# Written order instead of scheduled order: the queues of TensorE, ScalarE and VectorE in the MLP's stage of an attention and MLP kernel

## Chip, cores and metric

The kernel runs on one core of a Trainium2 chip. The metric is the device time of one execution in microseconds (us), the median of several runs. Half a per cent is about what runs of this kernel tell from no change.

Short names, as in the profile: PE is TensorE (matmuls), PEld its weight loads, ACT is ScalarE, DVE is VectorE, POOL is GpSimd, SP is SyncE, which issues the transfers (DMA).

## What is computed

Two attention blocks through 32 inducing points for each of 4 batches of 12480 rows of 128 values, and then an MLP with squared ReLU over all 49920 rows:

```python
def mab(q, kv):
    s = scale * (q @ kv.transpose(0, 2, 1))
    s = s - s.max(-1, keepdims=True)
    a = np.exp(s)
    a /= a.sum(-1, keepdims=True) + 1e-09
    return a @ kv
h = mab(I, x)                 # 32 inducing rows attend to all rows of x
x = mab(x, h)                 # each row of x attends to the 32 rows of h
hid = x.reshape(B * S, D) @ w_in          # 128 -> 2048
out = np.square(np.maximum(hid, 0)) @ w_out   # 2048 -> 128
```

## The kernel before

A row of the second attention is a mixture of the 32 rows of `h`, so the MLP's input has only 32 free values per row. The kernel uses that: per batch it prepares small matrices from `h`, `w_in` and `w_out`, and the MLP's 2048 hidden units become 512 squares of pair differences (four blocks of 128) and a linear part. An exact version for inputs on which this would not be close enough stands at the end, behind a switch, and is not taken here.

Per batch there are these pieces of work, each written as a Python generator whose `yield` ends a *step*:

- `first(b)`: the first attention. Seven groups of scores (four column groups side by side on PE, VectorE scales them into `sT` and takes maxima), the maximum's way across partitions (`mt`, `mb`, ending in `nb`), exponentials of `sT` on ACT, then for each of seven groups a transpose `en` on VectorE, a reduction `xm` over `xT` on VectorE, 30 small matmuls `hacc` on PE and a sum `hq` on VectorE; at the end `hs` and `ht`, which give `hT`.
- `prepare(b)`: 23 steps from `hT` to the MLP's matrices. PE: `hwv` (two halves of 8 blocks), `am`, `bc`, `R`, `pl`, `rb`, `cat`, `w` and four times `wq`; between any two of them VectorE has small work, and ACT evicts `hwv` and `wq` and casts `hws` (to `hw16`), `hwS` and `hot` (to `g4`).
- `second(b, G)`: the second attention for one of seven groups of columns: scores on PE, transpose and maximum on VectorE, a subtraction on POOL, the exponential on ACT, sum and reciprocal on VectorE, a multiplication on POOL, the transpose back, the narrowing to f16 on ACT or VectorE, a transfer to DRAM (`ad`) and back in another layout (`dT`).
- `squares(b, G)`: one small product per chunk (`sq`), squared on POOL (`zz`), which fills the last 32 rows of `dT`.
- 26 chunks of 480 columns: `up(j)` makes half j (two blocks of 128) of the pair differences on PE into `hp`; `lift(j)` squares that half on ACT into `g` (one instruction on 128 x 960); `down()` multiplies the four blocks of `g` by `w16` and adds the linear part into `po`, which ACT or VectorE evicts to `o`, and SP sends out.

PSUM holds two `hp` buffers (two banks each), two `po` and two for everything else (`att_psum`). Which of ACT and VectorE does an eviction is decided by `to_act` from two running sums of estimated work, `held`.

The program loops over the 104 chunks of all batches in order. After each half chunk, `background(k)` gives the next steps that are due: of `second` up to three groups ahead of the chunk, of `first` and `prepare` of the *next* batch so that they end with this batch's last chunks, and of `squares`. The order in which instructions are written is only a priority: a list scheduler puts each engine's queue in the order in which its own forecast has them ready. Before the loop, `first(0)` runs between the narrowing of the weights (`weights()`, a step of it at those steps of `first(0)` that `WHEN` lists), then `prepare(0)` with the first two groups of `second`.

Of the kernel before, what the change touches and what calls it, by code (L numbers as in the profile page):

```python
# [36 lines left out]
WHEN = (0, 2, 4, 8, 10, 12, 14)  # L37
# [3 lines left out]
def attend_then_relu2_mlp(ctx: ExitStack, tc: tile.TileContext, xn, xT, indT, w_in, w_out, outT):  # L41
# [20 lines left out]
    scale = 1.0 / math.sqrt(P)  # L62

# [15 lines left out]
    for k in range(2):  # L79
        nc.vector.tensor_reduce(fold[:, k], ident.rearrange("p (q i) -> p i q", q=4), axis=AX.X, op=ALU.add)  # L80
    rep = const.tile([P, 4, MI], F32, name="rep")
    nc.vector.tensor_copy(rep, fold[:, 0:1].broadcast_to([P, 4, MI]))
    ones = const.tile([1, P], F32, name="ones")
    nc.vector.memset(ones, 1.0)
    onec = const.tile([P, NF], F32, name="onec")
    nc.vector.memset(onec, 1.0)
# [3 lines left out]
    nc.vector.tensor_copy(slot, slot_i)  # L90

    late = const.tile([P, 1], F32, name="late")
    nc.vector.tensor_reduce(late, ident[:, 112:P], axis=AX.X, op=ALU.add)
    sgn = const.tile([P, NQ], F32, name="sgn")
    nc.vector.memset(sgn, -1.0)
    nc.vector.tensor_scalar(sgn[:, 3:4], late, 2.0, -1.0, op0=ALU.mult, op1=ALU.add)

    cut = const.tile([P, 1], F32, name="cut")
    nc.vector.tensor_reduce(cut, fold[:, 0, 0:16], axis=AX.X, op=ALU.add)
    nc.vector.tensor_scalar(cut, cut, -3e38, None, op0=ALU.mult)  # L100
    lessen = const.tile([P, 1], F32, name="lessen")
    nc.vector.memset(lessen, -(2.0 ** 14) / MI)
    part = const.tile([MI, 1], F32, name="part")
    nc.vector.memset(part, (2.0 ** 14) / MI)

    pairs = const.tile([P, NQ * P], F16, name="pairs")
    nc.vector.memset(pairs, 0.0)
    fold_f = fold.rearrange("p k i -> p (k i)")
    for s in range(1, 17):
        n = MI if s < 16 else 16  # L110
        nc.vector.tensor_tensor(
            pairs[0:64, MI * (s - 1):MI * (s - 1) + n], fold_f[0:64, 0:n], fold_f[0:64, s:s + n], op=ALU.subtract,
        )
    nc.vector.tensor_copy(pairs[0:64, 31 * 16:32 * 16], fold_f[0:64, 0:16])
# [11 lines left out]
    for k in range(2):  # L126
# [7 lines left out]
        nc.vector.memset(one.singles, 0.0)  # L134
        nc.vector.tensor_copy(one.singles[0:64, 0:16], fold[0:64, 0, 16:MI])
# [23 lines left out]
    def evac(dst, src, cols, by=None):  # L159

        if to_act(120 + 0.833 * cols, 110 + 1.042 * cols):
            if by is None:
                nc.scalar.copy(dst, src)
            else:
                nc.scalar.mul(dst, src, by)
        elif by is None:
            nc.vector.tensor_copy(dst, src)
        else:
            nc.vector.tensor_scalar(dst, src, by, None, op0=ALU.mult)
# [10 lines left out]
    def all_max(col, name):  # L180

        tp = att_psum(f"{name}_t")
        nc.tensor.transpose(tp[0:1, 0:P], col, ident)
        m = work.tile([1, 1], F32, tag="am_m", name=f"{name}_m")
        nc.vector.tensor_reduce(m, tp[0:1, 0:P], axis=AX.X, op=ALU.max)
        nc.vector.tensor_scalar(m, m, 2.0 ** -60, None, op0=ALU.max)
        yield
        bp = att_psum(f"{name}_b")
        nc.tensor.matmul(bp[:, 0:1], ones, m, start=True, stop=True)
        p2 = work.tile([P, 1], F32, tag="am_p", name=f"{name}_p", bufs=4)  # L190
        nc.vector.tensor_copy(p2, bp[:, 0:1])
        nc.vector.tensor_scalar(p2.bitcast(I32), p2.bitcast(I32), 0x7F800000, None, op0=ALU.bitwise_and)
# [7 lines left out]
    def narrow(dst, wd, name):  # L200
# [5 lines left out]
        nc.vector.tensor_scalar(a, hi, 3, 0x3FFFFFFF, op0=ALU.logical_shift_left, op1=ALU.bitwise_and)  # L206
        nc.vector.scalar_tensor_tensor(a, hi, 0xC0000000, a, op0=ALU.bitwise_and, op1=ALU.bitwise_or)
        nc.vector.tensor_scalar(m, a, 0xFF800000, None, op0=ALU.bitwise_and)
        nc.vector.scalar_tensor_tensor(r, lo, 2.0 ** -52, m.bitcast(F32), op0=ALU.mult, op1=ALU.mult)
        nc.vector.tensor_tensor(r, a.bitcast(F32), r, op=ALU.add)  # L210
        nc.vector.tensor_scalar(m, hi, 0x7FFFFFFF, None, op0=ALU.bitwise_and)
        nc.vector.scalar_tensor_tensor(dst, m, float(0x38100000), r, op0=ALU.is_ge, op1=ALU.mult)
# [3 lines left out]
    def prepare_w_out():  # L216
        m = small("wmax")
        nc.vector.tensor_reduce(m, wm4, axis=AX.X, op=ALU.max)
        p2 = yield from all_max(m, "wo")
        nc.vector.tensor_scalar(inv_t, p2, 2.0 ** -14, None, op0=ALU.mult)  # L220
        t = small("wt")
        nc.vector.reciprocal(t, inv_t)
        nc.scalar.mul(w_hi, wo_sb, t)
        yield
# [9 lines left out]
    def scores(ps, lhsT, xp, w):  # L234
        for q in range(4):
            nc.tensor.matmul(  # L236
# [3 lines left out]
    def first(b):  # L240
# [3 lines left out]
        nc.vector.memset(sT[:, NCH * TP:NCH * TP + 16], 0.0)  # L244
        mx = work.tile([P, NG], F32, tag="mx", name=f"mx_{b}")
        for G, w in enumerate(WID):
            if b:
                st.xp[G] = load_xT(b, G)
                yield
            ps = att_psum(f"s1_{b}_{G}")  # L250
            xg = st.xp[G]
            scores(ps, indT_sb, xg, w)
            held["dve"] += 150 + 1.042 * w
            nc.vector.tensor_scalar(
                sT[:, 480 * G:480 * G + w], ps[:, 0:w], scale, None, op0=ALU.mult, op1=ALU.max, accum_out=mx[:, G:G + 1],
            )
            yield

# [15 lines left out]
        xns = {h: load_xn(h) for h in range(XB)}  # L274
        m1 = small("m1")
        nc.vector.tensor_reduce(m1, mx, axis=AX.X, op=ALU.max)
        tp = att_psum(f"mt_{b}")
        nc.tensor.transpose(tp[0:1, 0:P], m1, ident)
        gm = work.tile([1, MI], F32, tag="gm", name=f"gm_{b}")
        nc.vector.tensor_reduce(gm, tp[0:1, 0:P].rearrange("a (q i) -> a i q", q=4), axis=AX.X, op=ALU.max)  # L280
        gm4 = work.tile([1, 4, MI], F32, tag="gm4", name=f"gm4_{b}")
        nc.vector.tensor_copy(gm4, gm.unsqueeze(1).broadcast_to([1, 4, MI]))
        yield
        bp = att_psum(f"mb_{b}")
        nc.tensor.matmul(bp[:, 0:1], gm4.rearrange("a q i -> a (q i)"), ones[:, 0:1], start=True, stop=True)
        nb = small("nb")
        nc.vector.tensor_scalar(nb, bp[:, 0:1], -1.0, None, op0=ALU.mult)  # L287
        yield

        def largest(G):  # L290
            held["dve"] += 60 + 1.042 * 4 * WID[G]
            nc.vector.tensor_reduce(  # L292
# [3 lines left out]
        def exp(G):  # L296
# [3 lines left out]
            nc.scalar.activation(s, s, AF.Exp, bias=nb, accum_out=zs[:, G:G + 1])  # L300
# [6 lines left out]
        for G, nb32 in enumerate(BLK):  # L307
            en = work.tile([P, 15, MI], F32, tag="en", name=f"en_{b}_{G}")
            held["dve"] += 110 + 1.042 * 32 * nb32
            nc.vector.transpose(  # L310
                en[:, 0:nb32].rearrange("p t i -> p (t i)"), sT[:, 480 * G:480 * G + 32 * nb32],
            )
# [3 lines left out]
            yield  # L316
            hacc = att_psum(f"hacc_{b}_{G}")
            for t in range(nb32):
# [4 lines left out]
                st.last = nc.tensor.matmul(  # L323
# [4 lines left out]
            if G == 0:  # L328
                nc.vector.tensor_copy(hq[:, 0:P], hacc[:, 0:P])
            else:  # L330
                nc.vector.tensor_tensor(hq[:, 0:P], hacc[:, 0:P], hq[:, 0:P], op=ALU.add)  # L331
            if G == NG - 1:
                nc.vector.tensor_reduce(hq[:, P:P + 1], zs, axis=AX.X, op=ALU.add)
            yield
        hs = att_psum(f"hs_{b}")
        nc.tensor.matmul(hs[:, 0:P + 1], rep.rearrange("p q i -> p (q i)"), hq, start=True, stop=True)
        zr = small("zr")
        nc.vector.tensor_scalar(zr, hs[:, P:P + 1], 1e-9, None, op0=ALU.add)
        nc.vector.reciprocal(zr, zr)
        nc.vector.tensor_scalar(st.hn, hs[:, 0:P], zr, None, op0=ALU.mult)  # L340
        yield
        ht = att_psum(f"ht_{b}")
        nc.tensor.transpose(ht[:, 0:P], st.hn, ident)
        nc.vector.tensor_copy(st.hT[:, 0:P], ht[:, 0:P])
        nc.vector.tensor_reduce(st.hT[:, P:P + 1], ht[:, 0:MI], axis=AX.X, op=ALU.add)
        nc.vector.tensor_scalar(st.hT[:, P:P + 1], st.hT[:, P:P + 1], 1.0 / MI, None, op0=ALU.mult)
        yield

    def second(b, G, again=False):
# [6 lines left out]
        if wb > w:  # L356
            nc.vector.memset(ps[:, w:wb], 0.0)  # L357
# [4 lines left out]
        nc.vector.transpose(ef[:, 0:wb], ps[:, 0:wb])  # L362
# [577 lines left out]
```

## Time and profile before

| | |
|---|---|
| time, median of 3 runs | 578.0 us (576.37 to 578.41) |
| the profiled execution's own time | 579.12 us |
| its span, first to last instruction | 577.3 us |
| mean granted TensorE clock | 0.869 of full speed |
| busy: PE, VectorE, ACT, POOL | 438.9, 365.3, 296.8, 83.4 us |
| weight loads (PEld, beside PE) | 204.5 us |

How to read it: one execution on the chip is profiled. Busy time is the sum of an engine's instructions; the granted clock is what the power and activity throttle allowed TensorE, 1.00 being full speed. A row of a group names the kernel's line, the engine, the operation, what it writes and reads, the count, the busy us and mean ns of one, and then the idle time of the engine just before these instructions and what ended it. In a row of the time order the first number is the start, the second the length, both in us; `x4` counts merged instructions.

### The profile page before, as it was taken

The page shows a single profiled execution, that of the slowest core. Times are in us where ns is not written, and L with a number is a line of the kernel's source. Part 1 is how long each engine was busy: PE and PEld are TensorE (multiplying, and loading weights), DVE is VectorE, ACT ScalarE, POOL GpSimd, SP SyncE. Part 2 cuts the span into 40 slices and gives each one's busy share as a digit, 9 for nine tenths or more (in the row PEclk, how much of TensorE's full clock was granted, in tenths as well). Part 3 has the DMA queues.
Part 4 walks back from the last instruction along what each step waited for, and adds up shares of the span by engine and source line. Part 5 has one row for each costly group of instructions (what it writes and reads, how often), then busy time and mean ns, then how long its engine had stood idle before and what let it go on. Part 6 is the DMA issues. An engine that isn't in the chain of part 4 may idle for free.

```text
span 577.3 us, 8820 instructions
## 1 busy us (share of the span) xinstructions
PE 438.9 (76%) x3083; PEld 204.5 (35%) x3083; DVE 365.3 (63%) x947; ACT 296.8 (51%) x419; POOL 83.4 (14%) x93
## 2 busy tenths in 40 slices
PE   1615465777798889769878899769777999897882
PEld 0014334522233536413333545313243555223330
DVE  6999758662555268997254298985534378767342
ACT  0030112437577266747875376628574476565771
POOL 0000011030211010242021021222011022422010
PEclk9999655997789569989889799969969599899997
DMA  8958715024528606565867535735866332334543
GB/s 322 399 214 277 277 69 154 1 86 155 179 80 305 199 20 226 172 182 167 280 226 230 178 102 186 270 104 145 311 211 190 107 105 72 97 126 130 168 132 131
DMA packets 64590, 100.82 MB, mean 175 GB/s; under 512 B 22800, under 2 KB 53776, under 8 KB 64528
## 3 DMA queue, kind: packets, MB, share of 16 engines
q1 hardware_dynamic: 64528, 100.08, 52.1%
q8 instruction: 28, 0.46, 0.3%
q14 instruction: 34, 0.28, 0.2%
HBM read 64.91 MB, written 31.95 MB: 168 GB/s over the span
## 4 chain that ended last, share of the span: by engine, by line
PE 44%; DVE 28%; ACT 13%; issue 6%; DMA 3%; POOL 3%; SPq 1%; POOLq 0%; ACTq 0%; DVEq 0%
PE po L654 10%; PE hp L639 9%; ACT g L648 8%; PE s L236 7%; DVE xm L292 5%; PE hwv L448 5%; PE hacc L323 4%; DVE G L605 3%; DMA outT_dram<-o 2%; PE po L655 2%; PE wq L611 2%; ACT o L658 2%; DVE e L362 2%; PE R L529 2%; DVE z L372 2%
## 5 line engine op out<-in xcount | busy, mean ns | idle before, releaser
L648 ACT ACTIVATE g<-hp 128x960 f16<-128x960 f32 x208 | 193.2, 970 | 87.9 <-PE hp L639 48.9
L639 PE MATMUL hp<-dT,pairs 96*128 96x480 f16 x416 | 122.0, 385 | 29.0 <-ACT g L648 28.1
L654 PE MATMUL po<-g,w 128*128 128x480 f16 x416 | 119.4, 399 | 16.1 <-ACT o L658 6.0
L368 POOL TENSOR_TENSOR e<-e,mx 128x480 f32<-128x480 f32 (+1 forms) x28 | 26.5, 947 | 334.8 <-DVE mx L364 222.8
L639 PEld LDWEIGHTS <-pairs 96*128 96x128 f16 x416 | 37.8, 99 | 97.6 <-issue 75.7
L654 PEld LDWEIGHTS <-w 128*128 128x128 f16 x416 | 41.1, 104 | 75.4 <-issue 43.9
L292 DVE TENSOR_REDUCE xm<-xp_False 128x1 f32<-128x1920 f32 (+1 forms) x28 | 55.7, 1989 | 5.3 <-DMA xp_False<-xT_dram 5.3
L658 ACT ACTIVATE o<-po,bias,osc 128x480 f32<-128x480 f32 x66 | 48.9, 753 | 18.9 <-PE po L655 7.1
L236 PE MATMUL s<-xp_False,indT_sb 128*32 128x480 f32 (+1 forms) x224 | 37.7, 743 | 20.5 <-DMA xp_False<-xT_dram 12.3
L323 PE MATMUL hacc<-xnb,en 128*32 128x128 f32 x784 | 39.2, 328 | 17.2 <-issue 9.3
L655 PE MATMUL po<-dT,lin 128*128 128x480 f16 x104 | 42.3, 408 | 2.7 <-DMA dT<-zz 2.7
L432 POOL TENSOR_TENSOR zz<-z 128x480 f16<-128x480 f32 (+1 forms) x28 | 28.9, 1030 | 87.8 <-DVE z L428 72.1
L660 DVE TENSOR_SCALAR o<-po,osc,bias 128x480 f32<-128x480 f32 x38 | 28.7, 767 | 18.0 <-DMA outT_dram<-o 6.8
L323 PEld LDWEIGHTS hacc<-xnb,en 128*32 128x32 f32 x784 | 26.7, 129 | 34.3 <-issue 20.1
L300 ACT ACTIVATE sT<-sT,nb 128x480 f32<-128x480 f32 (+1 forms) x28 | 18.2, 653 | 35.5 <-DVE nb L287 35.5
L236 PE MATMUL s<-xp_False,hT 128*32 128x480 f32 (+1 forms) x224 | 34.5, 628 | 2.1 <-DVE s L357 1.7
L375 POOL TENSOR_TENSOR e<-e,z 128x480 f32<-128x480 f32 (+1 forms) x28 | 27.6, 986 | 53.8 <-DVE z L374 48.6
L428 DVE TENSOR_SCALAR z<-sq,off,cut 128x480 f32<-128x480 f32 (+1 forms) x28 | 21.4, 764 | 21.8 <-PE sq L422 21.7
L605 DVE TENSOR_TENSOR G<-hwp,hw 128x512 f16<-128x512 f16 x64 | 30.1, 510 | 5.0 <-PE wq L611 4.7
L369 ACT ACTIVATE e<-e 128x480 f32<-128x480 f32 (+1 forms) x28 | 16.1, 574 | 31.6 <-POOL e L368 31.6
L362 DVE STREAM_TRANSPOSE e<-s 128x480 f32<-128x480 f32 (+1 forms) x28 | 18.0, 644 | 15.4 <-PE s L236 14.9
L331 DVE TENSOR_TENSOR hq<-hacc,hq 128x128 f32<-128x128 f32 x24 | 6.8, 284 | 33.0 <-PE hacc L323 33.0
(208 smaller groups left out, 498.6 us busy)
## 6 DMA issues: line engine op xcount, KB each, us to landing
outT_dram<-o SPq DMA_DIRECT2D x104, 240.0 KB, 2.2
xp_False<-xT_dram SPq DMA_DIRECT2D x24, 960.0 KB, 5.8
xnb<-xn_dram SPq DMA_DIRECT2D x28, 448.0 KB, 6.1
xnb<-xn_dram SPq DMA_DIRECT2D x24, 512.0 KB, 5.8
dT<-ad SPq DMA_DIRECT2D x72, 120.0 KB, 2.7
ad<-a SPq DMA_DIRECT2D x24, 240.0 KB, 2.7
dT<-zz SPq DMA_DIRECT2D x104, 30.0 KB, 1.9
wi<-w_in_dram SPq DMA_DIRECT2D x4, 512.0 KB, 5.4
```

The source lines that it names most:

```text
L236: nc.tensor.matmul(ps[32 * q:32 * q + 32, 0:w], lhsT, xp[:, w * q:w * q + w], start=True, stop=True,)
L292: nc.vector.tensor_reduce(st.xm[:, G:G + 1], st.xp[G], axis=AX.X, op=ALU.max, apply_absolute_value=True,)
L323: st.last = nc.tensor.matmul(hacc[32 * q:32 * q + 32, 0:P], en[:, t], xg[:, t % 8], start=t < 4, stop=t + 4 >= nb32,)
L362: nc.vector.transpose(ef[:, 0:wb], ps[:, 0:wb])
L432: nc.gpsimd.tensor_tensor(g[rows], zv[rows], zv[rows], op=ALU.mult)
L448: nc.tensor.matmul(ps[:, k * (MI + 1):(k + 1) * (MI + 1)], w_in_sb[:, f:f + P], st.hT[:, 96:P + 1], start=True, stop=True,)
L605: tt(g[:, :, MI * j:MI * j + n], hwp[:, :, 0:n], hw16f[:, :, s0:s0 + n], op=ALU.mult)
L639: nc.tensor.matmul(hp[:, i, 0:CH].rearrange("p (q t) -> p q t", q=4), pairs[0:96, (2 * j + i) * P:(2 * j + i + 1) * P], self.dT[0:96], sta ...
L648: nc.scalar.activation(self.g[:, 2 * j:2 * j + 2], self.hp.pop(j)[:, 0:2, 0:CH], AF.Square)
L654: nc.tensor.matmul(po[:, 0:CH], st.w16[:, i], self.g[:, i], start=i == 0, stop=False)
L655: nc.tensor.matmul(po[:, 0:CH].rearrange("p (q t) -> p q t", q=4), st.lin, self.dT, start=False, stop=True)
L658: nc.scalar.activation(o, po[:, 0:CH], AF.Identity, bias=st.bias, scale=st.osc)
```

## The change

The change does these things:

1. Every `nc.tensor`, `nc.scalar` and `nc.vector` call goes through a small class (`pe`, `act`, `dve`). From the loop over chunks on, it marks each instruction so that it stays behind the instruction written before it on its engine. POOL's and SP's queues stay with the scheduler. Nothing is computed differently.
2. `down` is given in two parts, two blocks of `g` each, one per half chunk; the linear part and the eviction are in the second.
3. In each half chunk the due steps are taken in turns from the three lists; every other one stands between `up` and `down`, the rest behind `down`.
4. Steps are cut elsewhere: `second` has six instead of four (POOL's subtraction alone, the transpose back alone), `first` has a transpose and the `hacc` before it in one step; `xT` is loaded three groups ahead (`LEAD`), the first `xn` loads stand before the last scores, `m1` and `cs` one step earlier. The numbers of steps (`N_...`) and `WHEN` follow.

```diff
-WHEN = (0, 2, 4, 8, 10, 12, 14)
+LEAD = 3
+KEPT = ("tensor", "scalar", "vector")
+WHEN = (0, 2, 4, 8, 10, 11, 12)
...
+    kept = set()
+    class Engine:
+        def __init__(self, name):
+            self.name, self.engine = name, getattr(nc, name)
+        def __getattr__(self, op):
+            def emit(*args, **kwargs):
+                ins = getattr(self.engine, op)(*args, **kwargs)
+                return tc.keep_in_program_order(ins) if self.name in kept else ins
+            return emit
+    pe, act, dve = Engine("tensor"), Engine("scalar"), Engine("vector")
...
     def first(b):
...
+        if b:
+            for G in range(LEAD):
+                st.xp[G] = load_xT(b, G)
+            yield
+        xns = {}
         for G, w in enumerate(WID):
-            if b:
-                st.xp[G] = load_xT(b, G)
-                yield
+            if b and G + LEAD < NG:
+                st.xp[G + LEAD] = load_xT(b, G + LEAD)
+            if G == NG - LEAD or G == NG - 1:
+                for h in range(XB):
+                    if (h < 2) == (G < NG - 1):
+                        xns[h] = load_xn(h)
             ps = att_psum(f"s1_{b}_{G}")
...
-        xns = {h: load_xn(h) for h in range(XB)}
-        m1 = small("m1")
...
+            if G == NG - 1:
+                m1 = small("m1")
+                dve.tensor_reduce(m1, mx, axis=AX.X, op=ALU.max)
+            yield
...
+        def turned(G):
             en = work.tile([P, 15, MI], F32, tag="en", name=f"en_{b}_{G}")
...
             if G + 2 < NG:
                 exp(G + 2)
             largest(G)
-            yield
+            return en
+        ens = {0: turned(0)}
+        yield
+        for G, nb32 in enumerate(BLK):
+            en = ens.pop(G)
             hacc = att_psum(f"hacc_{b}_{G}")
...
+            else:
+                ens[G + 1] = turned(G + 1)
             yield
...
     def second(b, G, again=False):
...
         nc.gpsimd.tensor_tensor(e[:, 0:t], e[:, 0:t], mx..., op=ALU.subtract)
-        nc.scalar.activation(e[:, 0:t], e[:, 0:t], AF.Exp, scale=scale)
+        yield
+        act.activation(e[:, 0:t], e[:, 0:t], AF.Exp, scale=scale)
...
+        dve.transpose(a[:, 0:wb], ef[:, 0:wb])
+        yield
...
-        def down(self):
+        def down(self, part):
             st = self.st
+            if part == 0:
+                self.po = ps_o.tile([P, 512], F32, tag="po", name=f"po_{self.b}_{self.c}")
+            po = self.po
+            for i in (2 * part, 2 * part + 1):
+                pe.matmul(po[:, 0:CH], st.w16[:, i], self.g[:, i], start=i == 0, stop=False)
+            if part == 0:
+                return
...
-    N_SECOND, N_SCORES, N_HEADS, N_PRE, N_SQ = 4, 2 * NG, 20, 23, 2
+    N_SECOND, N_SCORES, N_HEADS, N_PRE, N_SQ = 6, NG + 1, 14, 23, 2
...
-        give(1, nexts[1], 4)
+        give(1, nexts[1], 2)
...
     for j in (0, 1):
         chunks[0].up(j)
+    kept.update(KEPT)
...
         for j in (0, 1):
+            k += 1
+            steps = background(k)
             chunk.lift(j)
             if nxt:
                 nxt.up(j)
-            if j == 0 and n:
-                chunks[n - 1].down()
-            k += 1
-            background(k)
-    chunks[-1].down()
+            for gen in steps[0::2]:
+                next(gen, None)
+            if n:
+                chunks[n - 1].down(j)
+            for gen in steps[1::2]:
+                next(gen, None)
+    for j in (0, 1):
+        chunks[-1].down(j)
+    kept.clear()
```

In `background(k)`, `give(...)`, which ran the steps at once, becomes `due(...)`, which returns them as a list; the three lists (of `second`, of the next batch, of `squares`) are then merged in turns.

More of the change, by code (lines that the diff above doesn't have):

```diff
@@ L427, in squares @@
         held["dve"] += 110 + 1.042 * CH
-        nc.vector.tensor_scalar(z[rows], ps[rows, 0:CH], st.off[rows], cut[rows], op0=ALU.add, op1=ALU.max)
+        dve.tensor_scalar(z[rows], ps[rows, 0:CH], st.off[rows], cut[rows], op0=ALU.add, op1=ALU.max)
         yield
@@ L472, in prepare @@
         ps = att_psum(f"am_{b}")
-        nc.tensor.transpose(ps[0:1, 0:P], am, ident)
-        nc.tensor.matmul(ps[0:1, P:P + MI], xm, dh, start=True, stop=True)
+        pe.transpose(ps[0:1, 0:P], am, ident)
+        pe.matmul(ps[0:1, P:P + MI], xm, dh, start=True, stop=True)
         row = work.tile([1, 2], F32, tag="row", name=f"row_{b}")
-        nc.vector.tensor_reduce(row[:, 0:1], ps[0:1, 0:P], axis=AX.X, op=ALU.max)
-        nc.vector.tensor_reduce(row[:, 1:2], ps[0:1, P:P + MI], axis=AX.X, op=ALU.max)
+        dve.tensor_reduce(row[:, 0:1], ps[0:1, 0:P], axis=AX.X, op=ALU.max)
+        dve.tensor_reduce(row[:, 1:2], ps[0:1, P:P + MI], axis=AX.X, op=ALU.max)
         ts(row[:, 0:1], row[:, 0:1], 2.0 ** -60, None, op0=ALU.max)
@@ L481, in prepare @@
         ps = att_psum(f"bc_{b}")
-        nc.tensor.matmul(ps[:, 0:2], ones, row, start=True, stop=True)
+        pe.matmul(ps[:, 0:2], ones, row, start=True, stop=True)
         two = small("two", 2)
-        nc.vector.tensor_copy(two, ps[:, 0:2])
+        dve.tensor_copy(two, ps[:, 0:2])
         rho = two[:, 1:2]
@@ L489, in prepare @@
         ts(k2, p2, 2.0, None, op0=ALU.mult)
[L490 removed]
+        dve.reciprocal(s, k2)
         yield
@@ L496, in prepare @@
         for k in range(2):
-            nc.scalar.copy(hw16[:, :, k], hws)
+            act.copy(hw16[:, :, k], hws)
         hw16f = hw16.rearrange("p k q i -> p k (q i)")
@@ L707, in attend_then_relu2_mlp, with due, give @@
     given = {"ahead": 0, "sqs": 0, **{b: 0 for b in nexts}}
-    def give(what, gen, want):
-        while given[what] < want:
+    def due(what, gen, want):
+        steps = [gen] * max(0, want - given[what])
+        given[what] += len(steps)
+        return steps
+    def give(*args):
+        for gen in due(*args):
             next(gen, None)
-            given[what] += 1
     for n, _ in enumerate(prepare(0)):
```

313 lines of the change are left out of this document (154 added, 159 removed).

## Prediction

> **What bounds the kernel now.** I read the page's totals first, then the granted clock and the busy time by stage, then the costliest groups, and last the order of time around a few chunks. Columns of the stage rows: stretch and length in us, busy us (instructions) of PE, PEld, DVE, ACT, POOL, granted clock, DMA share, GB/s.
>
> ```profile
> span 577.3 us, 8820 instructions
> PE 438.9 (76%) x3083; PEld 204.5 (35%) x3083; DVE 365.3 (63%) x947; ACT 296.8 (51%) x419; POOL 83.4 (14%) x93
> 97.00:117.40 20.40, 16.72 (x167) 10.77 (x165) 11.37 (x49) 7.64 (x12) 0.00 (x0) 0.97 0.09 26
> 117.40:485.00 367.60, 310.45 (x2244) 143.27 (x2243) 220.66 (x588) 223.42 (x320) 58.26 (x61) 0.87 0.54 175
> 485.00:568.50 83.50, 70.06 (x345) 26.81 (x343) 51.26 (x100) 53.10 (x63) 19.56 (x20) 0.96 0.41 134
> L648 ACT ACTIVATE g<-hp 128x960 f16<-128x960 f32 x208 | 193.2, 970 | 87.9 <-PE hp L639 48.9
> L658 ACT ACTIVATE o<-po,bias,osc 128x480 f32<-128x480 f32 x66 | 48.9, 753 | 18.9 <-PE po L655 7.1
> L660 DVE TENSOR_SCALAR o<-po,osc,bias 128x480 f32<-128x480 f32 x38 | 28.7, 767 | 18.0 <-DMA outT_dram<-o 6.8
> PE hp L639 <- ACT g L648: 28.1, 56, 2.8
> 169.05 2.03 ACT sT L300 x6
> ```
>
> The profiled execution took 579.1 us for a span of 577.3; the runs' median is 578.0, so I take 0.7 off a span's sum plus the 1.8 around it. The MLP's stage runs from about 97 to 568.5: 471.5 us, in which PE is busy 16.7 + 310.5 + 70.1 = 397 us. So TensorE is the busiest engine in every stretch, and idles 74 us. Part of the 397 is a clock below full (0.87 over the long stretch). ACT (284 us in the three stretches) and VectorE (283) have a third of the stage free. Today the scheduler orders each engine's queue by its own forecast of times: it put six exponentials of `sT` back to back (169.05), and it evicts `o` wherever it fits. PE waits for `g` only 28.1 us in all.
>
> **The loop that the written order makes.** From the code: half j of chunk n issues lift(n,j) on ACT, then up(n+1,j) on PE, then every other background step, then half of down(n-1), then the other steps. `hp` has two buffers, so up(n+1,1) must wait for lift(n,1). In the second half PE's queue then holds up(n+1,1), steps, the second part of down(n-1). ACT's queue holds lift(n,1), the eviction of `o` of n-1, lift(n+1,0). With all queues kept, that eviction waits for PE, and lift(n+1,0) waits behind it, and PE's next up waits for that lift. This is one closed loop per chunk whenever ACT evicts `o`. Rows for its legs, all at full clock (columns: start us, us, instruction, the last number the count):
>
> ```profile
> 263.48 0.98 PE L639 MATMUL hp<-dT,pairs 96*128 96x480 f16 x4
> 264.10 1.83 ACT L648 ACTIVATE g<-hp 128x960 f16<-128x960 f32 x2 [0.65 <-PE hp L639]
> 265.11 0.37 PE L655 MATMUL po<-dT,lin 128*128 128x480 f16 x1
> 272.41 1.39 ACT L658 ACTIVATE o<-po,bias,osc 128x480 f32<-128x480 f32 x2
> 280.41 0.56 PE L639 MATMUL hp<-dT,pairs 96*128 96x480 f16 x2 [0.41 <-ACT g L648]
> 554.77 4.52 ACT L648 ACTIVATE g<-hp 128x960 f16<-128x960 f32 x5 [0.35 <-PE hp L639]
> ```
>
> A 480-column matmul streams in 0.2 us (0.98 for four with a tail of 0.17). From the end of lift(n,1): handoff 0.05 (the first pair of 263.48 ends at 264.05, `g` starts at 264.10; the same is taken for the other direction), up 0.4, three matmuls of down 0.6 and tail 0.17, handoff 0.05, `o` 0.64 until the next ACT instruction (1.39 for two of 0.75), lift 0.97, and the chunk's other lift 0.87 behind it (1.83 for two): 3.75 us. Of that PE streams 1.8. A chunk whose `o` VectorE evicts has no such loop: two lifts at 4.52 / 5, and a handoff, 1.85 us.
>
> Which engine evicts is decided by two running sums in the code (`held`), which I added up in both orders: 66 evictions on ACT before, as the page counts, and 67 after. So bare chunks cost 67 x 3.75 + 37 x 1.85 = 251 + 69 = 320 us.
>
> **The background beside it.** PE work of a step adds to the loop whole, because PE's order is serial from one lift to the next. The exception is what stands behind the second part of down: it fills the wait for `o` and lift (0.17 + 0.05 + 0.64 + 0.97 + 0.05, about 1.88).
>
> ```profile
> 196.80 7.01 PE L448 MATMUL hwv<-hT,w_in_sb 128*128 128x33 f32 x32
> 265.41 1.01 PE L236 MATMUL s<-xp_False,hT 128*32 128x480 f32 x8
> 268.28 0.39 PE L422 MATMUL sq<-dT,singles 96*32 96x480 f16 x4
> 297.18 1.01 PE hacc L323 x16
> 299.11 0.82 PE hacc L323 x14
> 467.89 3.61 PE R L529 x32
> 475.11 1.12 PE rb L560 x32
> 477.51 1.00 PE w L596 x16
> 480.03 0.91 PE wq L611 x16
> ```
>
> The rows without a tile's shape are of the chain that ended last, in order of time. Per batch, with a last group of half size: scores of the next batch 6.5 x 0.95 (1.01 less its tail), scores of `second` the same, `hacc` 6 x 1.83 + 0.5, `hwv` 7.0, R 3.6, rb 1.1, w4 1.0, four wq 3.7, squares 2.6, nine single small matmuls at about 0.4 each 3.6: 46.5 us. Going through the steps' numbers, five of them land behind the second part of down: hacc2 1.83, hacc6 0.5, hwv1 1.88, w4 1.0, cm 0.3, so 5.5 are hidden and 41 are not. Three batches give 123; what is left of `second` and the squares for the last batch gives 6. Together 129.
>
> **Waits on ACT's and PE's own queues inside the steps.** A step that gives ACT something which needs PE or VectorE of the same half holds up lift(n,1) or lift(n+1,0), and PE's next up with it.
>
> ```profile
> 116.02 0.37 ACT L165 ACTIVATE w<-wq,tsg 128x128 f16<-128x128 f32 x1 [2.52 <-PE wq L611]
> 200.44 0.38 ACT L163 COPY hwv<-hwv 128x264 f32<-128x264 f32 x1 [7.28 <-PE hwv L448]
> 210.22 0.48 DVE L494 TENSOR_SCALAR hws<-hwv,s 128x512 f32<-128x512 f32 x1
> 210.73 1.14 ACT L497 CAST hw<-hws 128x512 f16<-128x512 f32 x2 [0.21 <-DVE hws L494]
> 211.11 0.68 DVE L362 STREAM_TRANSPOSE e<-s 128x480 f32<-128x480 f32 x1 [0.42 <-PE s L236]
> 211.91 0.65 DVE L364 TENSOR_REDUCE mx<-e 128x15 f32<-128x480 f32 x1
> 212.70 0.77 DVE L428 TENSOR_SCALAR z<-sq,off,cut 128x480 f32<-128x480 f32 x1
> 222.19 0.18 PE L539 MATMUL pl<-ident,rm 32*1 32x32 f32 x1
> 223.23 0.42 DVE L552 TENSOR_TENSOR hot<-slot,inc 128x256 f32<-128x256 f32 x1
> 224.28 0.40 ACT L555 CAST g<-hot 128x256 f16<-128x256 f32 x1
> L605 DVE TENSOR_TENSOR G<-hwp,hw 128x512 f16<-128x512 f16 x64 | 30.1, 510 | 5.0 <-PE wq L611 4.7
> L292 DVE TENSOR_REDUCE xm<-xp_False 128x1 f32<-128x1920 f32 (+1 forms) x28 | 55.7, 1989 | 5.3 <-DMA xp_False<-xT_dram 5.3
> L310 DVE STREAM_TRANSPOSE en<-sT 128x480 f32<-128x480 f32 x24 | 15.8, 666 | 0.4 <-ACT sT L300 0.4
> ```
>
> Per batch: the step with `hws` falls in a half whose scores and square come first. VectorE does transpose, max and z before `hws`, then ACT its two casts and the lift. From the half's start that is 1.4 + 2.0 + 0.6 + 1.1 + 0.95 = 6.05 us, where PE is done at 2.2: 3.9 lost. The step pl: 1.46 us from its transpose to `hot`'s end (222.19 to 223.65), then cast 0.4 and lift 0.97: 2.8. The two `hwv` evictions, 0.38 + 0.97 and a handoff: 2 x 1.4. Three of four wq evictions likewise 3 x 1.4 = 4.2. wq0 waits for its four G's (2.0, behind a step's 1.4 on ACT and VectorE) where PE comes 1.3 into the half: 1.9. ht and bc 1.4. In the heads, from the start of hacc(G) VectorE needs the reduction of `xT` (2.0), the sum (0.3, an estimate: less than half of the transpose, for a quarter of its columns) and the next transpose (0.67), 3.0 us, before hacc(G+1) may start; hacc3 and hacc4 lie 1.83 + 0.4 apart, so 0.75 is lost, and as much again where a step of `second` stands between: 1.6, the least sure. Sum 18.6, and 56 for three batches. The bounds: 0, if VectorE runs ahead enough, to twice that, if its own kept queue is late by as much again.
>
> **The clock.** By rows, PE may be busy and yet slow: the first row below is `hwv` alone, the second the last batch's end, with chunks only.
>
> ```profile
> 450.00:455.00 5.00, 5.00 (x24) 4.62 (x24) 0.03 (x1) 0.76 (x2) 0.00 (x0) 0.50 0.02 7
> 540.00:568.50 28.50, 23.34 (x107) 9.71 (x106) 11.99 (x17) 18.11 (x20) 2.50 (x3) 1.00 0.47 157
> ```
>
> The first lies on the weight-bound `hwv`, which slows the chunk around it: I add one chunk at half clock per batch (9 x 0.2 = 1.8), 5 us. Bounds: 0, as in the last batch, and 56, the 397 busy us of the stage less 104 x 1.8 = 187 and 154 of background (three batches of 46.5, the last batch's 6, about 8 of the first preparation's end); some of that is only matmuls' tails. A rule speaks against the change here: the Trainium skill, "TensorE: Matmul & The Clock Gate", Part 1, has an idle window of about 3.4 us halve the clock and a busy one of that length restore it. By that rule the 3.9 us wait of the `hws` step would cost another 1.7 us, by estimate, in each of three batches, and the sum would be 5 higher, 633; no row here shows the clock just after so long a wait in this loop.
>
> **Everything else, and the start and end.** The loads of `xT` three groups ahead and of `xn` before the last scores: 0, covered by at least two chunks of loop; between -2 and +5 by the 5.8 us from issue to landing, since SP's queue holds them with the dT and `o` transfers. The copy of `cs` and the maximum m1 one step earlier: -1. The finer steps of `second`: no instruction more, and POOL's two multiplications keep their order on a queue that is 14% busy. The transfer of `o` is issued half a chunk later on SP: 0, except once at the end, where the last chunk has both halves anyway. WHEN: 10, 11, 12 name the same places in the new, merged steps as 10, 12, 14 before; 0. The loop takes over when the last w16 column block is scaled, 116.4 (row at 116.02). Two chunks with 2.3 us of steps lie before that, -9.8. From the last lift to the span's end I take 11.
>
> Sum: 116.4 - 9.8 + 320 + 129 + 56 + 5 + 11 = 628 of span, 629 with what lies around it, 628 by the runs' measure: 9% slower. In one sentence: PE loses most of the idle time that the scheduler's order had filled with chunk work, 67 times about 1.88 us, and gains back only the bursts.
>
> **The rivals.**
> 1. *The queues run ahead and the steps' waits vanish* (faster). VectorE and ACT have a third of the stage free, and steps lie a half apart; if each result is there when the next kept instruction wants it, the 56 and the 5 are 0 and the time is 567. Against: ACT's casts follow `hws` by 0.21 us even now. It ends faster when these waits stay under 8 us in all, and within half a per cent up to 14.
> 2. *The kept order is close to what the scheduler gave* (the change does little): 578. For: 263 to 267 above reads up, lift, down, scores, much as written. Against: the exponentials of 169.05 in a row cannot stand in the written order.
> 3. *The waits compound*: VectorE stands behind an eviction, PE behind VectorE, the clock halves more often. Twice the 56, and half of the clock's bound: 628 + 56 + 28 - 5, about 707. For: VectorE has 13 steps per batch with PE on both sides.
>
> **How the numbers follow.** The likeliest, 628, has 0.67; rival 1 0.20 (my loop is strict, but its legs may each be 0.1 too long, and 67 x 0.2 is 13 us), rival 2 0.05, rival 3 0.08. Half a per cent, 2.9 us, is about what runs of this kernel (576.4 to 578.4) can tell. Faster 0.20, same 0.05, slower 0.75. The likeliest's own range is 600 to 656, from the waits' 56 at half and at half as much again. To leave out no more than 2 in 10, the range reaches to the first rival's 567 and to 662.
>
> **What would show it.** Right: ACT's wait for `po` before `o` grows from 7.1 us to 60 or more, PE's wait for `g` before `hp` from 28.1 to over 120, PE's busy time in the stage falls with a clock above 0.9, chunks of the last batch fall from 83.5 / 26 = 3.2 us to about 2.1, and the first three batches grow from 122 to about 150 us each. Each step: exponentials at most two in a row, idle ACT before the casts of `hws` and `hot`. Wrong: chunks with `o` on ACT at 3.3 us or less, or no wait of ACT for `po`, which would mean the loop isn't closed; or hacc, R and wq lying mostly within the wait for `g`.

## The result, and the profile after

The changed kernel takes 735.8 us (median of 4 runs, 732.3 to 743.7) against 577.4 for the kernel before on the same chip: 1.272 times as long (95% interval 1.266 to 1.279). The slowest of the four runs, 743.7, is left out of that ratio. The forecast was 628, range 567 to 662. The direction was right and the loop it rests on is in the trace; the size was 108 us short.

From the page of the changed kernel: span, busy times, the granted clock in 40 slices, and two groups (busy us, mean ns of one, idle time before them and what ended it). All calls of PE, ACT and VectorE now go through one helper, so every line of theirs is L75 and the tiles tell the work apart.

```profile
span 735.4 us, 8806 instructions
...
PE 489.1 (67%) x3083; PEld 233.5 (32%) x3083; DVE 370.9 (50%) x947; ACT 295.0 (40%) x419; POOL 82.2 (11%) x93
...
PEclk9555556886965686589797567699977567799998
...
L75 PE MATMUL hp<-dT,pairs 96*128 96x480 f16 x416 | 142.5, 430 | 158.5 <-ACT g L75 158.3
...
L75 ACT ACTIVATE o<-po,bias,osc 128x480 f32<-128x480 f32 x67 | 50.3, 751 | 195.5 <-issue 157.6
```

The same 3083 matmuls keep PE busy for 489.1 us where it was 438.9; ACT and VectorE have the work they had. PE's wait for `g` rose from 28.1 to 158.3 us. ACT's idle time before `o`, 18.9 us in the kernel before, is 195.5, and the row puts most of it down to "issue": what released it is not in the records. The order of time shows what it is. A stretch at full clock, ACT and PE only:

```profile
319.96 0.56 PE L75 MATMUL hp<-dT,pairs 96*128 96x480 f16 x2 [1.75 <-ACT g L75]
...
320.37 0.57 PE L75 MATMUL po<-g,w 128*128 128x480 f16 x2
...
320.86 1.01 PE L75 MATMUL s<-xp_False,indT_sb 128*32 128x480 f32 x8
...
321.81 0.58 PE L75 MATMUL hp<-dT,pairs 96*128 96x480 f16 x2
...
322.23 0.57 PE L75 MATMUL po<-g,w 128*128 128x480 f16 x2
...
322.63 0.36 PE L75 MATMUL po<-dT,lin 128*128 128x480 f16 x1
...
323.09 0.75 ACT L75 ACTIVATE o<-po,bias,osc 128x480 f32<-128x480 f32 x1 [1.82 <-issue]
...
323.74 1.82 ACT L75 ACTIVATE g<-hp 128x960 f16<-128x960 f32 x2
...
324.75 0.56 PE L75 MATMUL hp<-dT,pairs 96*128 96x480 f16 x2 [1.75 <-ACT g L75]
```

This is the forecast's loop: the last matmul into `po` ends at 322.99, `o` starts 0.10 later, the lift behind it at 323.74, and PE's next up at 324.75 after 1.75 us of waiting (forecast 1.88). From up to up it takes 4.79 us, of which the eight scores between add about 1.0; that leaves 3.8 for the bare chunk (forecast 3.75).

The stage by batch, from each batch's first lift to the next one's, each border within 0.3 us (columns as in the prediction):

```profile
117.40:311.00 193.60, 132.09 (x779) 57.96 (x779) 82.63 (x212) 80.62 (x118) 23.30 (x24) 0.73 0.38 123
311.00:490.10 179.10, 123.36 (x765) 56.44 (x765) 78.30 (x198) 76.84 (x112) 19.29 (x20) 0.75 0.42 134
490.10:657.30 167.20, 117.49 (x771) 56.67 (x770) 84.23 (x214) 72.66 (x105) 20.27 (x21) 0.78 0.33 106
657.30:722.40 65.10, 54.38 (x283) 23.34 (x282) 38.83 (x69) 49.50 (x57) 13.97 (x15) 0.97 0.46 147
```

The forecast had the first lift at 106.6 (116.4 - 9.8), 456 us for the first three batches, 54 for the last and 11 behind the last lift. Measured: 117.7, 539.9, 65.1 and 13. So of the 108 us, 11 lie at the start, 84 in the three batches, 11 in the last batch and 2 at the end. The clock of those three batches is 0.73 to 0.78, where the forecast had it above 0.9, and PE's busy time rose where the forecast had it fall.

### The profile page after: what moved, and what is told of

It is laid out like the page before. It is cut to its first block, busy times and chain, and to the rows that moved or that the text cites. A ratio compares the mean times of both kernels' runs of the same rounds, so it can differ in the third digit from the quotient of the medians.

```text
span 735.4 us, 8806 instructions
## 1 busy us (share of the span) xinstructions
PE 489.1 (67%) x3083; PEld 233.5 (32%) x3083; DVE 370.9 (50%) x947; ACT 295.0 (40%) x419; POOL 82.2 (11%) x93
## 5 line engine op out<-in xcount | busy, mean ns | idle before, releaser
L75 PE MATMUL hp<-dT,pairs 96*128 96x480 f16 x416 | 142.5, 430 | 158.5 <-ACT g L75 158.3
L75 ACT ACTIVATE g<-hp 128x960 f16<-128x960 f32 x208 | 194.9, 966 | 6.2 <-PE hp L75 5.5
L75 PE MATMUL po<-g,w 128*128 128x480 f16 x416 | 144.6, 436 | 0.7 <-DVE o L75 0.7
L75 ACT ACTIVATE o<-po,bias,osc 128x480 f32<-128x480 f32 x67 | 50.3, 751 | 195.5 <-issue 157.6
L75 PEld LDWEIGHTS <-pairs 96*128 96x128 f16 x416 | 40.9, 106 | 234.3 <-issue 212.5
L75 PEld LDWEIGHTS <-w 128*128 128x128 f16 x416 | 41.5, 109 | 68.6 <-issue 44.3
L75 DVE TENSOR_REDUCE xm<-xp_False 128x1 f32<-128x1920 f32 (+1 forms) x28 | 55.3, 1974 | 0.0
L75 PE MATMUL hacc<-xnb,en 128*32 128x128 f32 x784 | 39.5, 345 | 20.4 <-issue 12.5
L75 PE MATMUL s<-xp_False,indT_sb 128*32 128x480 f32 (+1 forms) x224 | 35.6, 687 | 20.1 <-DMA xp_False<-xT_dram 12.2
L75 DVE SCALAR_TENSOR_TENSOR a<-a,lessen,a 128x480 f16<-128x480 f32 (+1 forms) x28 | 19.0, 680 | 52.3 <-ACT a L75 52.0
L75 DVE STREAM_TRANSPOSE e<-s 128x480 f32<-128x480 f32 (+1 forms) x28 | 18.1, 648 | 53.1 <-PE s L75 53.1
L75 PE MATMUL po<-dT,lin 128*128 128x480 f16 x104 | 44.7, 430 | 0.0
L75 DVE TENSOR_SCALAR o<-po,osc,bias 128x480 f32<-128x480 f32 x37 | 28.3, 766 | 25.8 <-PE po L75 18.6
L75 PEld LDWEIGHTS hacc<-xnb,en 128*32 128x32 f32 x784 | 28.7, 137 | 35.0 <-issue 18.3
L75 DVE TENSOR_SCALAR_CACHE_REDUCE sT<-s 128x480 f32<-128x480 f32 (+1 forms) x28 | 17.2, 616 | 40.3 <-PE s L75 40.2
L75 PE MATMUL s<-xp_False,hT 128*32 128x480 f32 (+1 forms) x224 | 34.1, 687 | 4.2 <-DVE s L75 4.2
L75 ACT ACTIVATE sT<-sT,nb 128x480 f32<-128x480 f32 (+1 forms) x28 | 18.3, 656 | 40.6 <-DVE nb L75 40.6
L75 PE MATMUL wq<-w_hi,G 128*128 128x128 f16 x256 | 25.3, 276 | 7.8 <-DVE G L75 7.5
L75 PEld LDWEIGHTS hwv<-hT,w_in_sb 128*128 128x128 f32 x128 | 28.9, 333 | 3.4 <-issue 2.3
```

The source lines that it names most:

```text
L75: ins = getattr(self.engine, op)(*args, **kwargs)
```

## The experiments

All edits are of the changed kernel (735.8 us). "Before" is the kernel before on the same chip, between 577.4 and 579.7 us in these comparisons.

**Which queue is at fault.** Four kernels change only the set of kept queues.

```diff
-KEPT = ("tensor", "scalar", "vector")
+KEPT = ("tensor", "vector")     # ACT left to the scheduler
```

> The changed kernel with only TensorE's and VectorE's queues in written order; ACT's is the scheduler's again. Theory loop: ACT can square the next half before an eviction whose matmuls are late, so PE's wait for g falls from 158 us to under 60, and the time to 570 to 620. Rival VectorE: time above 690, the waits for VectorE's results stay.

580.0 us, 1.006 (1.001 to 1.011) of before.

```diff
+KEPT = ()                       # no queue kept
```

> The changed kernel with no queue kept: half chunks, finer steps, steps in turns and the earlier loads remain. Theory loop and clock: the written order is the whole loss, so 565 to 595, the clock near 0.87. Rival: the half chunks and the spread steps themselves cost, so 620 or more.

571.1 us, 0.984 (0.980 to 0.988). So the finer steps, the half chunks and the earlier loads cost nothing when the scheduler orders them, and the kept order is the whole loss.

```diff
+KEPT = ("tensor", "scalar")     # VectorE left to the scheduler
```

> PE's and ACT's queues kept, VectorE's left to the scheduler. Loop theory: little changes, 705 to 740, since the loop runs over ACT and PE alone. Rival 3 of the prediction (VectorE's kept order makes waits compound): 56 us or more go at full clock and more by the clock, 660 or less.

725.0 us, 1.254 (1.238 to 1.270): VectorE's kept queue is worth about 11 us of 736, and the intervals of the two ratios still touch.

```diff
+KEPT = ("scalar",)              # PE and VectorE left to the scheduler
```

> ACT's queue alone kept, PE's and VectorE's left to the scheduler. If the loss is PE's order as well as ACT's (the loop is closed by the second part of down standing behind up and steps on PE), the scheduler can put steps into PE's wait and the time is 590 to 670; if ACT's order alone is enough, since lift(n+1,0) stands behind the eviction of o whatever PE does, it is above 690.

599.2 us, 1.037 (1.023 to 1.051). The row of the list of waits for PE behind `g`, first of PE and ACT kept, then of ACT alone:

```profile
PE hp L75 <- ACT g L75: 143.6, 93, 4.3
```

```profile
PE hp L75 <- ACT g L75: 36.3, 39, 6.5
```

Against 571 with none kept, ACT alone costs 28 us, PE with VectorE 9, but PE with ACT 154. The loss belongs to the pair, as a closed loop over two queues would have it: with either one left free most of the loss is gone.

**Opening the loop.** The eviction of `o` goes to VectorE, or stays on ACT half a chunk later, behind the lift that stood behind it. All three queues stay kept.

```diff
-            if to_act(220 + 0.833 * CH, 110 + 1.042 * CH):
+            held["dve"] += 110 + 1.042 * CH
+            if False:
```

> The changed kernel with every eviction of o on VectorE (67 of 104 were on ACT). Theory loop (lift waits on ACT behind an eviction that waits for PE): the bare chunk falls from 3.75 to about 1.9 us, 67 x 1.9 = 127 us less, and more where PE's denser work brings the clock back: 560 to 610. Rival (VectorE's own kept queue is the bound): VectorE gets 50 us more work and its evictions wait for PE as ACT's did, so 700 or more.

669.7 us, 1.154 (1.147 to 1.161), between the two expected outcomes. PE's wait for `g` falls from 158.3 to 88.5 us, but VectorE, whose queue is kept as well, now waits 60.4 us for PE before `o` (18.6 in the changed kernel), and ACT's wait for POOL before the exponentials of `second` rises from 18.2 to 56.5 us. So this edit opens one loop and pays with other waits.

```diff
+        def evict(self):        # o and its transfer, split from down(1)
...
                 nxt.up(j)
+            if j == 0 and n > 1:
+                chunks[n - 2].evict()
...
```

> All three queues kept as in the changed kernel, but the eviction of o (and its transfer) is written half a chunk later, after the lift that stood behind it: ACT's order is lift(n,1), lift(n+1,0), o of n-1. Nothing else moves. Loop theory: the eviction's matmuls are done by then, so neither ACT's wait before o (157.6 us put down to issue and 37.1 to po in the changed kernel) nor PE's wait for g behind it (158.3) is left in full; a bare chunk with o on ACT falls from 3.75 to ACT's own 2 x 0.9 + 0.75 = 2.6 or less. That is 67 x 1.1 = 77 us at least at full clock, and a busier PE drops its clock less often: 600 to 660 us, PE's wait for g under 80. Rival (ACT's steps with their PE and VectorE inputs are what the time goes to, wherever o stands): 705 or more, the waits before o turning up before hwv, w, hw and the lifts.

632.1 us, 1.094 (1.078 to 1.109): 104 us less for one instruction per chunk moved by half a chunk. A chunk of it with `o` on ACT, in order of time:

```profile
300.06 0.56 PE L75 MATMUL hp<-dT,pairs 96*128 96x480 f16 x2 [0.43 <-ACT g L75]
...
300.88 0.36 PE L75 MATMUL po<-dT,lin 128*128 128x480 f16 x1
...
301.28 0.75 ACT L75 ACTIVATE o<-po,bias,osc 128x480 f32<-128x480 f32 x1 [0.40 <-PE po L75]
...
301.93 1.82 ACT L75 ACTIVATE g<-hp 128x960 f16<-128x960 f32 x2
...
302.94 0.56 PE L75 MATMUL hp<-dT,pairs 96*128 96x480 f16 x2 [0.34 <-ACT g L75]
```

Up to up now takes 2.88 us (with eight scores of half the width between), and PE waits 0.34 to 0.43 for `g` instead of 1.75. PE's wait for `g` over the whole kernel is 84.2 us (158.3), a little above the 80 expected. That the loop is where the largest part of the time goes is thereby shown. Part of the 104 us comes by way of the clock: over the first three batches PE is busy at half speed for 130 us, where it was 206 in the changed kernel.

**Waits inside the steps.** Of ACT's instructions only the lifts and `o` keep the written order; first in the changed kernel, then with `o` later as well.

```diff
+    acs = nc.scalar             # for evac, the casts and exponentials of the steps
-            act.activation(s, s, AF.Exp, bias=nb, accum_out=zs[:, G:G + 1])
+            acs.activation(s, s, AF.Exp, bias=nb, accum_out=zs[:, G:G + 1])
...
```

> PE's and VectorE's queues kept; of ACT's only the lifts and the evictions of o keep the written order, the steps' ACT instructions (evictions of hwv and wq, casts, exponentials) go where the scheduler puts them. Loop theory: the loop over o stays, so PE's wait for g stays above 110 us and the time at 670 to 725 (the 56 us of waits inside steps that I forecast can go, and some clock with them). Rival (the steps' ACT instructions cost the time): 620 or less.

714.1 us, 1.235 (1.218 to 1.252): 22 us less, and the wait for `g` stays at 137.0 us. The loop does not need the steps. The 22 us are a net figure: left to the scheduler, the exponentials of `second` wait for POOL for 76.4 us, 18.2 in the changed kernel.

> The eviction of o half a chunk later, as in the run with that alone (632.1 us), and the steps' ACT instructions left to the scheduler, as in the run with that alone (714.1, 21.7 under the changed kernel). If the two costs stand beside each other: 632 - 22 = 610, between 600 and 620. If the loop had hidden the waits inside the steps (they pass while PE waits for the loop anyway), more goes: 580 to 600. If those 21.7 us came from the loop's clock alone, nothing goes: 625 or more.

626.8 us, 1.087 (1.080 to 1.094): only 5 us under the 632.1, which is not clear of the noise. So most of the 22 came by way of the loop, and freeing the steps on ACT is worth 5 us net at most once it is open.

**The clock.** Six matmuls per chunk that nobody reads are written into the next `po` behind the second half's up and steps, before its own sum starts; first in all batches, then in the first three only.

```diff
+        def fill(self):
+            self.po = ps_o.tile([P, 512], F32, tag="po", name=f"po_{self.b}_{self.c}")
+            for _ in range(FILL):                          # then: FILL if self.b < 3 else 0
+                pe.matmul(self.po[:, 0:CH], self.st.w16[:, 0], self.g[:, 0], start=True, stop=True)
...
-            if part == 0:
-                self.po = ps_o.tile([P, 512], F32, tag="po", name=f"po_{self.b}_{self.c}")
...
+            if j:
+                chunk.fill()
```

> The changed kernel with six more matmuls of 480 columns per chunk on PE, behind the second half's steps, where PE waits for the eviction of o and the next lift (1.88 us by the sum). They write the next chunk's po, which the chunk's own first matmul then starts anew, so nothing is computed differently. Theory clock (PE's share of the time fell below what holds full speed, so matmuls run at half speed for about 290 us of the stage): more PE work makes it faster; granted clock from 0.75 to 0.88 or more, time from 736 to 640 to 670. Theory waits (VectorE's and ACT's waits were priced too low, and the clock only follows): the waits stay where they are, time within 2% of 736 or up to 60 us above it.

709.1 us, 1.222 (1.205 to 1.239), mean clock 0.934 in the profiled run. This is outside both expected ranges. The first three batches fell from 539.9 to 487.3 us, but the last batch, which has next to no such wait to fill (one of its 26 evictions is on ACT), rose from 65.1 to 84.7 us.

> The changed kernel with six extra matmuls per chunk, written into po before its own sum starts and overwritten by it, in the first three batches only; they add 1.2 us of PE work per chunk into the wait for o and the lift. Clock theory (much of my 5 us term for the clock is really 50 us or more, because a chunk whose PE is under about half busy in 3.4 us drops to half speed): the first three batches as with the filler everywhere (487 us where the changed kernel had 540), the last batch back from 84.7 to 65: 680 to 695, mean clock 0.9 or more. Rival (the clock follows from the waits and costs nothing of its own): 735 or more, since 78 x 1.2 us of PE work is added.

691.7 us, 1.199 (1.192 to 1.207). The first three batches, by stage:

```profile
117.00:290.00 173.00, 141.93 (x935) 65.71 (x935) 83.00 (x212) 80.57 (x118) 23.29 (x24) 0.89 0.44 143
290.00:452.80 162.80, 135.10 (x915) 64.50 (x915) 77.94 (x198) 76.72 (x112) 18.59 (x20) 0.91 0.44 142
452.80:610.00 157.20, 132.46 (x926) 63.61 (x926) 84.92 (x214) 72.62 (x105) 20.26 (x22) 0.93 0.35 112
```

78 x 6 matmuls of 0.2 us are 94 us of added PE work, and the kernel is 44 us *faster*: 493 us for the three batches instead of 540, at a clock of 0.89 to 0.93. Besides `po` being taken earlier nothing else was changed, so at least 44 us of the changed kernel are the clock's, beyond what the filler itself may cost.

**The start.** The queues are kept from the third chunk on.

```diff
-    kept.update(KEPT)
...
+        if n == 2:
+            kept.update(KEPT)
```

> The changed kernel with the queues kept from the third chunk on and not from the first lift on. My credit of 9.8 us for two chunks before the last w16 block supposed that lifts may go ahead of that block's scaling on ACT; in the changed kernel the first lift stands at 117.5, behind it. If that is the reason: the first lift comes back to about 100 and 8 to 12 us go, 722 to 729. If the start is set by something else (dT, the scheduler's order): 733 to 738.

736.4 us, 1.277 (1.268 to 1.286): no gain, against the expectation. The last scaling of `w16` and the first lift, in the changed kernel and then here:

```profile
117.43 0.37 ACT L75 ACTIVATE w<-wq,tsg 128x128 f16<-128x128 f32 x1 [3.35 <-PE wq L75]
...
117.69 1.82 ACT L75 ACTIVATE g<-hp 128x960 f16<-128x960 f32 x2
```

```profile
101.02 0.97 ACT L75 ACTIVATE g<-hp 128x960 f16<-128x960 f32 x1 [2.46 <-PE hp L75]
...
117.26 0.37 ACT L75 ACTIVATE w<-wq,tsg 128x128 f16<-128x128 f32 x1 [3.35 <-PE wq L75]
```

The lift does come back to 101, but the first batch then takes 205.0 us instead of 193.6: only four lifts run before the last block of `w16` is scaled, which comes at the same time as before, and the sums of the first chunks wait for each block.

**The last batch.** Two empty steps are put between POOL's subtraction in `second` and the exponential; first in the changed kernel, then with `o` later as well.

```diff
         nc.gpsimd.tensor_tensor(e[:, 0:t], e[:, 0:t], mx..., op=ALU.subtract)
         yield
+        yield
+        yield
         act.activation(e[:, 0:t], e[:, 0:t], AF.Exp, scale=scale)
...
-    N_SECOND, ... = 6, ...
+    N_SECOND, ... = 8, ...
```

> The changed kernel with two empty steps put between POOL's subtraction in second and ACT's exponential behind it (8 steps a group), so that the exponential is written about 1.7 halves later. In the last batch of the changed kernel ACT waits 10.0 us for POOL before four exponentials, and the lifts stand behind them; my sum had no such wait. If that is why the last batch took 65.1 us and not 54: it falls to 55 to 60 and the time to 718 to 731. Rival (the last batch is bound by something else, such as the transfers): 65 again, 733 or more.

707.1 us, 1.226 (1.214 to 1.238). The changed kernel's last batch has the rows of the first block; the second block is its whole wait of this kind there:

```profile
675.43 0.60 ACT L75 ACTIVATE e<-e 128x480 f32<-128x480 f32 x1 [3.51 <-POOL e L400]
675.94 2.67 ACT L75 ACTIVATE g<-hp 128x960 f16<-128x960 f32 x3
...
676.94 0.56 PE L75 MATMUL hp<-dT,pairs 96*128 96x480 f16 x2 [2.60 <-ACT g L75]
```

```profile
ACT e L75 <- POOL e L400: 10.0, 4, 3.6
```

With the empty steps the exponential starts without a wait, but for one of 1.4 us in the last batch:

```profile
639.58 0.62 ACT L75 ACTIVATE e<-e 128x480 f32<-128x480 f32 x1
```

The stage row of the last batch is then:

```profile
631.80:690.40 58.60, 52.90 (x283) 22.73 (x281) 40.20 (x69) 49.12 (x57) 13.99 (x15) 1.00 0.51 163
```

The last batch falls from 65.1 to 58.6 us, as expected; the whole falls by 29, more than the 5 to 18 expected. The rest lies in the first batch (179.1 us instead of 193.6), at the start (first lift at 112.3) and 6 us in the other two batches. Why the first batch gains 14 was not tried apart, as all steps of `second` are shifted there too; its trace has PE busy at half speed for 63 us instead of 82, which would be some 9 of the 14.

> The eviction of o half a chunk later (632.1 us with that alone) and the exponential two steps later. Both loops that hold up ACT's lifts are then out of the last batch: 55 to 58 us for it, and 618 to 627 in all. If the exponential's wait only takes the place of another one: 630 or more.

617.2 us, 1.068 (1.053 to 1.082); last batch 60.1 us, 2 above the expected range. The edit is worth 29 us in the changed kernel and 15 once the loop over `o` is open, so about half of it seems to have come by way of that loop.

**Can the written order help the scheduler?** With no queue kept, the version of 571.1 us again, and then the two edits above on it.

> The finer steps, half chunks, earlier loads and finer interleaving, with no queue kept: the version that came out fastest (571.1 us, ratio 0.984) again, with more rounds. Its order as written, handed to the scheduler, gives it more choice of matmuls to fill PE's waits: 568 to 574, ratio 0.98 to 0.99. If the first look was luck: 575 to 580.

572.3 us in 12 runs, 0.992 (0.989 to 0.995). Together with the first comparison it is about 1% faster than before: the best version found here.

> No queue kept, and the exponential two steps later. The kernel of before had ACT wait 31.6 us for POOL before 19 exponentials, so the scheduler places them too early by its own forecast; a later place in the order of writing gives it less reason to: 560 to 572. If it pulls the exponentials ahead whatever the order of writing: 569 to 575, as without.

578.2 us, 1.000 (0.996 to 1.005).

> No queue kept, and the eviction of o half a chunk later in the order of writing. The scheduler sorts by its own forecast, and nothing waits behind o by the written order: 568 to 576, no change from the version without. If the written order is what it follows, ACT's waits before o shrink and the time falls to 560 to 567.

586.6 us, 1.015 (1.003 to 1.026). Both expectations missed: what opens a loop in the kept order makes the scheduled one 1 to 2.5% slower. The reason stays open; it shows that the written order still matters to the scheduler's result, and that a good place in one regime is no guide to the other.

## Why the prediction was right or wrong

**The loop, 320 us: right.** The place, the legs and the size (3.8 for 3.75, PE's wait 1.75 for 1.88) are as forecast; ACT's wait before `o` passed the 60 us named as the sign, and PE's wait for `g` the 120. Opening it takes 104 us off.

**The clock, 5 us (bounds 0 to 56): the step that failed.** I took the last batch, chunks alone at 1.00, as the row nearest to the new stage, and let only `hwv` slow it. But in that row PE is busy for 23.34 of 28.50 us, 82%. By the forecast's own numbers PE streams 1.8 of a loop's 3.75 us, 48%, and after stretches about that busy the granted clock falls. The trace grants the clock in stretches of 3.41 us; the changed kernel's rows for ten of them (PE's busy time is the first number behind the length, the granted clock the third from the end):

```profile
322.72:326.13 3.41, 1.66 (x14) 0.46 (x12) 0.88 (x3) 2.47 (x3) 0.99 (x1) 1.00 0.36 139
326.13:329.55 3.42, 3.04 (x13) 0.74 (x6) 1.26 (x3) 0.00 (x0) 0.00 (x0) 0.50 0.00 0
329.55:332.96 3.41, 1.75 (x12) 0.45 (x11) 0.72 (x1) 3.05 (x4) 0.00 (x0) 1.00 0.19 74
332.96:336.37 3.41, 1.66 (x11) 0.60 (x7) 0.67 (x2) 2.03 (x3) 0.00 (x0) 1.00 0.33 119
336.37:339.79 3.42, 3.42 (x19) 0.67 (x22) 1.31 (x3) 0.44 (x1) 0.00 (x0) 0.50 0.68 158
339.79:343.20 3.41, 2.02 (x13) 0.54 (x10) 1.38 (x4) 1.30 (x2) 1.94 (x2) 1.00 0.36 124
...
346.61:350.03 3.42, 1.69 (x14) 0.58 (x14) 0.69 (x4) 2.47 (x3) 0.99 (x1) 1.00 0.19 72
350.03:353.44 3.41, 1.74 (x5) 0.54 (x4) 1.06 (x4) 1.58 (x3) 0.00 (x0) 0.50 0.00 0
353.44:356.85 3.41, 3.33 (x9) 1.26 (x9) 1.21 (x3) 2.85 (x5) 0.00 (x0) 0.50 0.39 144
356.85:360.27 3.42, 3.33 (x23) 1.19 (x22) 2.35 (x4) 0.45 (x1) 0.10 (x1) 1.00 0.37 103
```

Full-speed stretches with PE busy for 1.66, 1.66 and 1.69 us are followed by half speed, those with 1.75 and 2.02 by full speed; half-speed stretches with 3.04, 3.42 and 3.33 are followed by full speed, the one with 1.74 is not. In the first three batches the changed kernel spends 270 us at half speed, with PE busy in 206 of them (summed over these stretches in the trace). Half of that, 103 us, is by estimate what the clock adds to PE's work, if all of it runs twice as fast at full speed. Before it was 99 and 89 us, so 44. Not all of the 103 is missing from the forecast: its 7.0 us for `hwv` were read at half speed. The first row is the changed kernel's half of `hwv` at a granted clock of 0.50, the second the filler kernel's at 1.00:

```profile
211.80 3.46 PE L75 MATMUL hwv<-hT,w_in_sb 128*128 128x33 f32 x16
```

```profile
204.77 1.87 PE L76 MATMUL hwv<-hT,w_in_sb 128*128 128x33 f32 x16
```

So about 3 us per batch, 10 in all, were already in the background's 129, and the clock's own term had 5. That leaves 88 us of clock that the forecast did not have, by estimate, against the 84 missing in these batches. The forecast's upper bound, 56, was read from the kernel before and could not hold for a busy share that the change itself lowers. The filler kernel has 88 us at half speed, 83 of them busy, and is 47 us faster in these batches: a part of the price, measured. The Trainium skill ("TensorE: Matmul & The Clock Gate", Part 1) names an idle window, in its table of the two states, as what halves the clock; the length of its window agrees with these stretches of 3.41 us, but here the windows that cost the clock were about half busy. The rule, read strictly, gave 633; the measurement decides.

**Waits inside steps, 56 us: too high, and one missing.** ACT does wait before the casts of `hws` (18.4 us, 4 times) and `hot` (26.4, 4 times), the first preparation's 1.4 and 2.4 included. But of the 18.6 us per batch 13.7 were ACT's (the casts and the evictions of `hwv` and `wq`), 41 for three batches, and freeing all the steps on ACT takes only 22 us off with the loop closed and 5 with it open, net of new waits for POOL. And the sum had no term for ACT's exponential of `second`, which stands behind POOL in the written order: 10.0 us in the last batch, 18.2 in all. I went through the steps by the engines whose queues are kept, and passed over POOL, whose queue isn't. In the last batch taking it away was worth 6.5 of the 11 us missing.

**The start, -9.8 us: wrong.** I let two chunks run ahead of the last `w16` block because it could be done; in the written order the lift stands behind that block's scaling, and where it doesn't, the stage gains nothing. The 11 us missing at the start are the credit and 1.3 us.

**The rivals.** Rival 1 (the steps' waits vanish) was partly true of ACT's steps, and small beside the clock. Rival 2 (written order close to the scheduler's) is excluded by 736 against 571 for one and the same text. Rival 3 (707) named the clock, with half of its bound, but gave the waits to VectorE, and VectorE's kept queue is worth 11 us. At 0.08 it was given too little: a forecast of a loop with PE busy for half of the time already holds its clock.

**Left open.** The terms don't add up one by one: 88 us of clock and 11 + 11 + 2 elsewhere are 112 against 108 missing. The 88 is an estimate that puts every slow matmul on the path that bounds the time; what the experiments show of it is the filler's 44, and how much of the rest the overpriced waits of the steps hide is not told apart. Nor is all of what keeps the kernel with both loops opened (617) 45 us above the changed kernel's text with no queue kept (572). Part of it is the clock: in the first three batches the one has PE busy at half speed for 109 us, the other for 57, which would be 26 of the 45.

## What to carry to other kernels

Before fixing the order of two engines' queues, write down for each engine what stands between an instruction and the one that its partner waits for: a single eviction between a matmul's end and the next lift closed a loop, and moving it by half a chunk was worth 104 us. Fix one queue at a time: here ACT's alone cost 28 us, PE's with VectorE's 9, and ACT's with PE's 154. And price a new wait on TensorE twice, once for itself and once for the clock, when it takes PE's busy share in a few microseconds down to about half.

## What the runs showed of the hardware

In the trace of the changed kernel the clock was granted in stretches of 3.41 us, at full or half speed only. From the first lift to the last, the full-speed stretches that were followed by half speed had PE busy for 0.14 to 0.53 of their time (24 stretches, median 0.45), those followed by full speed 0.49 to 1.0 (73 stretches). From half speed it came back only after stretches with 0.81 or more (25 stretches, median 1.0), and 55, median 0.63, stayed. A busy stretch did not always bring it back: 16 of the 55 had 0.81 or more as well.

The way down and the way back thus lie apart, and an estimate from the forecast's legs says what that does to the loop. At full speed PE streams 1.8 of 3.75 us, 0.48, and the clock falls. At half speed it streams 3.6 us and the rest, 1.95, stays, so it is busy for 3.6 of 5.55, or 0.65. That is near the 0.63 of the stretches that stayed and below all that came back, so by these figures a bare loop would not get out of half speed by itself. Work that nobody reads, put into the wait, made the kernel 6% faster (691.7 for 735.8), which fits.
